# Two changes in a planner's hints: when the first batch's last z tiles are let go, and how soon a block's gate matmuls may run

## The chip, the cores and the metric

The kernel runs on one core of a Trainium2 chip. The metric is the device time of one execution, in microseconds; the median of the runs counts.

## The reference

Attention with a squared-ReLU score is multiplied by `u`, and its rows go through a top-1 mixture of experts with a capacity.

```python
scores = (1 / S) * z @ z.T                # B=8, S=3072, d_qk=64
attn = maximum(scores, 0) ** 2
x = (u * (attn @ v)).reshape(B * S, D)    # D=256
logits = x @ w_gate                       # E=8 experts
expert_idx = argmax(logits, axis=1); gate_w = softmax(logits)[expert_idx]
# each expert takes its first cap = 768 rows, in the order of the tokens
h = maximum(disp @ w1, 0)                 # F=1024
y = h @ w2
out[i] = gate_w[i] * y[expert_idx[i], pos[i]] if kept, else 0
```

## The kernel before

**Work.** Since an expert takes only 768 rows, the kernel computes the attention of the first 14 blocks of 512 rows (`NB0`); blocks 0 to 5 are the first batch, 6 to 11 the second, 12 and half of 13 the third. A flag `more` says whether an expert is still short of rows; only then the second half of block 13, and what follows, is computed. In the runs here that branch isn't taken.

**A block** goes over 12 *pairs* of 128 keys. For each pair six matmuls give the scores (L867, tile `sc`, made for two pairs at a time), ScalarE takes ReLU and square (L884, L889), VectorE splits the result in a high and a low float16 part (L893, L902, tile `hl`), and 24 matmuls sum it with `v` (L993, tile `acc`). The scores are symmetric: what a later block needs again is written to DRAM (`kept`, L914) and loaded transposed (`ld`, L840).

**Key tiles.** The scores read `zz`, which holds z^T as high and low parts. For the first batch, tiles 0 to 11 (three groups of four) are made on TensorE: split by ScalarE and VectorE (L401, L404, L405), turned (L416), copied out (L422). Pairs 4 and 5 of block 0 read group 2. Tiles 12 to 23, read from pair 6 on, go another way: loaded a second time (`zlate`, L440), split six tiles at a time (`z_wide`: L449 on ScalarE, L452 on VectorE), turned by two DMA transposes (L456), and the two halves swapped by two more DMAs (L464).

**A block's route.** When a block's sums are done (L943, `x`), VectorE scales its rows (L651 and what follows), they are split (L663, L666) and turned by DMA (L674, `xt`); 16 gate matmuls (L681, `lg`) give the logits, VectorE takes the argmax (L692 to L697), five small matmuls count (L702 to L708, `cum`), VectorE makes slots, counts and the gate weight (L738 to L748, L721 to L726), and GpSimd scatters the rows to `disp` with four indirect DMAs (L84). For block 13 it is half of all that.

**Experts.** For a slab of rows, `fxt` is loaded transposed from `disp` by SP (L1088), L1132 makes the hidden layer (`hps`), L1117 and L1118 split it, L1154 multiplies by w2 (`yps`), L1160 scales, and GpSimd scatters the rows to `out` (L84). Expert 0 comes in slabs of 512, 128 and 128 rows, the others in one of 768. The first two slabs of expert 0 are loaded while block 12 runs. After the 512 rows, all engines read `more` (L1264) and pass the branch of L1265; behind it GpSimd runs one instruction that replaces the semaphore counts of the scatters that were skipped. The third slab and expert 1's are loaded after that.

**What sets the order.** Each engine works through its instructions in the order written. That order is made at build time: `Chain` holds stages of work for other engines, and between the matmuls of TensorE `weave` emits from each chain what fits. A chain isn't touched before its `gate` is in `done`; `("pair", p)` is set when the sums of pair p begin. A chain of rank -2 may put work on ScalarE and VectorE at any time. One of rank -1 may do so before pair 3 only where the engine's planned backlog is at most 0.2 us. Chains of lower rank come first. A chain's item for TensorE is emitted when the planner's clock has passed `ready + lag`:

```python
            if eng == "PE":
                return self.ready + self.lag <= now
...
                if self.rank < 0:
                    return self.rank < -1 or ("pair", 3) in done or t - now <= 0.2
```

`lag` is `LAG` = 4.5 (us of the planner) for the routes of all blocks but the last ones. The planner's microseconds are not measured times.

Of the kernel before, what the change touches and what calls it, by code (L numbers as in the profile page):

```python
# [26 lines left out]
def attention_moe_kernel(ctx: ExitStack, tc: tile.TileContext, u, v, z, w_gate, w1, w2, out, cap):  # L27
# [6 lines left out]
    JT = S // P  # L34
# [110 lines left out]
    def warm_up(n):  # L145

        t = ps.tile([P, BLK], F32, tag="acc", name="warm", bufs=3)
        for _ in range(n):
            op("PE", 0.2155)
            nc.tensor.matmul(t, lhsT=ones, rhs=ones.unsqueeze(1).to_broadcast([P, BLK // P, P]), start=True, stop=True)  # L150
# [22 lines left out]
    LAG = 4.5  # L173
# [4 lines left out]
    done = {}  # L178
# [10 lines left out]
    def op(eng, cost, dep=0.0):  # L189
        start = max(clk[eng], dep + HOP)  # L190
        if eng in ("SP", "XB"):
            start = max(clk["SP"], dep + HOP)
            clk["SP"] = start + (0.5 if eng == "SP" else max(1.2, 0.3 + cost))
            clk["DMA"] = max(clk["DMA"], start + 1.4) + cost
            return clk["DMA"] + 1.0
        clk[eng] = start + cost
        return clk[eng]
# [118 lines left out]
    def tag():  # L316
        uid[0] += 1
        return uid[0]
# [12 lines left out]
    def prepare(bt, first=False):  # L331
# [102 lines left out]
        ZW = 6  # L434

        NT = 3 * 4 if first else 0
# [5 lines left out]
        def z_wide(t0):  # L442
            st = Bag()
            k = min(ZW, JT - t0)
            src = (lambda: bt.zlate[:, t0 - NT:t0 - NT + k]) if first else (lambda: bt.zraw[:, t0:t0 + k])

            def hi():
                st.zhl = sb.tile([P, ZW, 2, DQ], F16, tag="zhl", name="zhl", bufs=3)
                nc.scalar.activation(st.zhl[:, 0:k, 0, :], src(), AF.Copy, scale=bt.zs)  # L449

            def lo():
                nc.vector.scalar_tensor_tensor(out=st.zhl[:, 0:k, 1, :], in0=src(), scalar=bt.zs,  # L452
                                               in1=st.zhl[:, 0:k, 0, :], op0=ALU.mult, op1=ALU.subtract)

            def tr():
                nc.sync.dma_start_transpose(  # L456
                    out=bt.zz[:, 0, t0 * P:(t0 + k) * P].rearrange("p (t q) -> p t q", q=P),
                    in_=st.zhl[:, 0:k].rearrange("p t h d -> p (t h d)"))

            return [[("ACT", 0.5, hi, None)], [("DVE", 0.48, lo, None)], [("XB", 0.68, tr, None)]]  # L460

        def z_swap(h):
            def f():
                nc.sync.dma_start(out=bt.zz[DQ * (1 - h):DQ * (2 - h), 1, NT * P:],  # L464
                                  in_=bt.zz[DQ * h:DQ * (h + 1), 0, NT * P:])
                if h:
                    for g in range(NT // 4, ZG):
                        done[key("z", g)] = clk["DMA"] + 1.0
            return ("SP", 1.2, f, key("z", NT // 4) if h else None)
# [28 lines left out]
        def v_piece(t0, k):  # L498
            o, i, a = slice(t0, t0 + k), t0 // 4, t0 % 4

            def hi():
                nc.scalar.activation(bt.v2[:, o, 0, :], bt.vraw[i][:, a:a + k], AF.Copy, scale=bt.vs)

            def lo():
                nc.vector.scalar_tensor_tensor(out=bt.v2[:, o, 1, :], in0=bt.vraw[i][:, a:a + k], scalar=bt.vs,
                                               in1=bt.v2[:, o, 0, :], op0=ALU.mult, op1=ALU.subtract)
                for j in range(t0 + 2, t0 + k, 2):
                    done[key("v", j // 2)] = clk["DVE"]

            return [[("ACT", 0.19 + 0.21 * k, hi, None)], [("DVE", 0.06 + 0.285 * k, lo, key("v", t0 // 2) if t0 + k > t0 // 2 * 2 + 1 else None)]]  # L510
# [12 lines left out]
        def pipe(groups):  # L523

            n = max(len(g) + i for i, g in enumerate(groups))
            return [[it for i, g in enumerate(groups) if 0 <= s - i < len(g) for it in g[s - i]] for s in range(n)]

        if first:
# [5 lines left out]
            late = op("SP", 2.0)  # L534
# [23 lines left out]
        def need_max(k, n):  # L558
            return max(done[key(k, i)] for i in range(n))
# [13 lines left out]
        def go(c, n=1):  # L573
            for _ in range(n):
                assert c.item() is not None
                c.emit()
# [16 lines left out]
        def to_sums(follow):  # L593

            G[1] = Chain(z_group(1), -2, done[key("s")])
            go(A[2])
            go(follow[0], 3)
            go(A[3])
            go(follow[0], 2)
            go(G[1])  # L600
            go(A[4])
            go(follow[1], 2)
            go(A[6])
            go(G[1])
            go(A[5])
            warm_up(14)
            go(G[1])
            warm_up(8)
            vr = Chain([[("DVE", 0.2, v_red, None)], [("POOL", 0.4, v_all, None)], [("DVE", 0.6, v_bits, key("vs"))]], -2,
                       need_max("m", NM))  # L610
            go(vr, 2)
            go(G[1], 2)
            go(vr)
            for t, k in ((0, 1), (1, 1), (2, 2)):
                V[t] = Chain(v_piece(t, k), -2, done[key("vs")])
            go(V[0])
            go(V[1])
            go(V[0])
            go(V[1])
            go(follow[1])  # L620
            go(V[2])
            go(follow[1], 2)
            go(V[2])
            Chain(z_group(2), -1, done[key("s")], gate=("pair", 0))
            Chain(pipe([z_wide(t0) for t0 in range(NT, JT, ZW)]) + [[z_swap(0), z_swap(1)]], -1, late, gate=("pair", 1))
            for i in range(2, JT // 2):
                Chain(v_piece(2 * i, 2), -2, done[key("vs")], gate=("pair", i - 2))

# [181 lines left out]
    def attention(blocks, hook):  # L810

        NP = len(blocks) * NPAIR
        prs, acc, xs, ut, sct, sq, corner = {}, {}, {}, {}, {}, {}, {}
# [132 lines left out]
        def start_route(n, rid):  # L946
            bt, _, _, cc = blocks[n]
            keys = [(aid, "x", n, h) for h in range(cc // 2)]
            watchers.append((lambda: all(k in done for k in keys), lambda: route(
                xs.pop(n), bt, max(done[k] for k in keys), LAG if n < len(blocks) - 2 else 0.5, cc, rid)))  # L950

        loads_to(1)
        bt = blocks[0][0]
# [6 lines left out]
        for p in range(NP):  # L960
            n, g = divmod(p, NPAIR)
            bt, ib, c0, cc = blocks[n]
# [8 lines left out]
            for c in range(cc):  # L971
# [7 lines left out]
                if g == 0 and c % 2 == 0:  # L979

                    k = bank[0] - 3
# [17 lines left out]
            if g == NPAIR - 1:  # L999
                need(bt.key("f"), "init")  # L1000
                acc.pop(n)
                ut.pop(n)
                rid = tag()
                last_route[0] = [(rid, "sc", c) for c in range(cc)], (rid, "cnt")
                start_route(n, rid)
# [202 lines left out]
    with tc.manual_schedule():  # L1208
# [4 lines left out]
        for b, bt in bats.items():  # L1213
            n = min(BPB, NB0 - b * BPB)
# [58 lines left out]
        blocks = [(bats[n // BPB], n % BPB, 0, CC if n < NB0 - 1 else CC // 2) for n in range(NB0)]  # L1273
# [59 lines left out]
```

## Time and profile before

| | |
|---|---|
| three runs | 799.09, 800.66, 807.9 us |
| median | 800.66 us |
| profiled execution | 804.33 us |
| its span, first to last instruction | 802.6 us |
| TensorE busy (matmuls) | 778.2 us, 97% of the span |
| VectorE, ScalarE, GpSimd busy | 493.0, 402.9, 115.9 us |

The attention ends at about 538 us of the span, the experts fill the rest. The profiled execution is 1.7 us longer than its span and 3.7 us above the median.

### The profile page before, as it was taken

Reading aid. Unit: us, or ns where it says so; the run is one execution under the profiler, and the core shown is the slowest. Engines: PE = TensorE matmul, PEld = TensorE weight load, DVE = VectorE, ACT = ScalarE, POOL = GpSimd, SP = SyncE. Lnnn points to the kernel's source line nnn. Section 1 sums busy time; section 2 is a strip of 40 time slices with the busy share of each in tenths; the row PEclk is TensorE's granted clock in tenths of the full one; section 3 lists DMA queues with packets and bytes.
Section 4 is the critical chain, followed back from the end, with each engine's and each line's share of the span. In section 5 each row is a group of like instructions: output and inputs, shape, how many; then the busy total and the mean of one; then the engine's idle time right before and its main releaser. Section 6 shows DMA issues by size and latency. Waiting matters only on the chain. (4 is left out here: it accounts for less than half of the span.)

```text
span 802.6 us, 17029 instructions
## 1 busy us (share of the span) xinstructions
PE 778.2 (97%) x6857; PEld 607.8 (76%) x6857; DVE 493.0 (61%) x1080; ACT 402.9 (50%) x692; POOL 115.9 (14%) x122
## 2 busy tenths in 40 slices
PE   8899999999999999999999999998999999999996
PEld 3587878788877777888688877866776877867865
DVE  6877888453526979874525269885674473564540
ACT  6877565322216748452413058553664464564541
POOL 0000010120102010101101010104121312312202
PEclk9999999999999999999999999999999999999998
DMA  7499999999998997889699989861997846845001
GB/s 216 140 221 283 243 210 238 184 246 177 223 192 206 279 232 228 193 195 227 160 223 208 195 203 253 285 182 43 198 329 266 294 131 260 233 153 170 27 15 44
DMA packets 287069, 160.60 MB, mean 200 GB/s; under 512 B 227341, under 2 KB 253274, under 8 KB 286976
## 3 DMA queue, kind: packets, MB, share of 16 engines
q1 hardware_dynamic: 282080, 146.58, 74.1%
q0 software_dynamic: 4896, 12.79, 4.9%
q8 instruction: 57, 0.93, 0.5%
q14 instruction: 36, 0.29, 0.1%
HBM read 36.25 MB, written 71.46 MB: 134 GB/s over the span
## 5 line engine op out<-in xcount | busy, mean ns | idle before, releaser
L993 PE MATMUL acc<-v,hl 128*128 128x256 f16 x2280 | 259.5, 273 | 0.7 <-DVE hl L902 0.4
L993 PEld LDWEIGHTS <-hl 128*128 128x128 f16 x2280 | 219.7, 98 | 34.9 <-issue 4.6
L884 ACT ACTIVATE r<-sc 128x512 f32<-128x512 f32 (+1 forms) x212 | 105.6, 550 | 151.8 <-PE sc L867 150.1
L993 PE MATMUL acc<-v,ld 128*128 128x256 f16 x1464 | 167.9, 274 | 4.1 <-DMA ld<-kept 2.8
L993 PEld LDWEIGHTS <-ld 128*128 128x128 f16 x1464 | 141.9, 98 | 26.8 <-issue 6.3
L1132 PE MATMUL hps<-fxt,wt 128*128 128x384 f16 (+2 forms) x816 | 128.1, 320 | 3.8 <-PEq L1265 2.4
L1154 PE MATMUL yps<-wt,hh 128*128 128x256 f16 x1152 | 128.0, 273 | 0.0
L1118 DVE SCALAR_TENSOR_TENSOR hh<-hps,hh 128x384 f16<-128x384 f32 (+2 forms) x136 | 71.1, 532 | 90.6 <-ACT hh L1117 89.5
L1154 PEld LDWEIGHTS <-hh 128*128 128x128 f16 x1152 | 112.5, 98 | 14.1
L902 DVE TENSOR_TENSOR hl<-a,hl 128x1024 f16<-128x1024 f32 (+1 forms) x106 | 118.2, 1115 | 3.6
L1132 PEld LDWEIGHTS <-wt 128*128 128x128 f16 x816 | 77.2, 99 | 52.6 <-issue 4.4
L84 POOL DMA_INDIRECT disp<-xr,slot x54 | 56.5, 1045 | 336.8 <-ACT r L884 129.3
L889 ACT ACTIVATE a<-r 128x1024 f32<-128x1024 f32 (+1 forms) x106 | 102.6, 968 | 2.5
L893 DVE CAST hl<-a 128x1024 f16<-128x1024 f32 (+1 forms) x106 | 67.6, 638 | 55.3 <-ACT a L889 55.1
L1117 ACT ACTIVATE hh<-hps 128x384 f16<-128x384 f32 (+2 forms) x136 | 63.2, 470 | 51.6 <-PE hps L1132 50.6
L867 PE MATMUL sc<-zz 64*128 64x512 f16 (+1 forms) x636 | 72.0, 356 | 2.6 <-DMA zz<-zz 1.9
L84 POOL DMA_INDIRECT out<-ys,sid x48 | 53.1, 1107 | 128.0 <-ACT ys L1160 85.3
L1160 ACT ACTIVATE ys<-yps,sg 128x256 f32<-128x256 f32 x48 | 22.7, 473 | 76.1 <-PE yps L1154 69.9
L663 ACT ACTIVATE xr<-x,rsr 128x256 f16<-128x256 f32 x54 | 25.2, 502 | 68.9 <-DVE rsr L60 66.2
L867 PEld LDWEIGHTS <-zz 64*128 64x128 f16 x636 | 26.9, 94 | 36.4 <-issue 10.7
L943 DVE TENSOR_TENSOR x<-acc,u 128x512 f32<-128x512 f32 x27 | 18.6, 689 | 46.8 <-PE acc L993 43.2
L1061 DVE SCALAR_TENSOR_TENSOR wt<-wraw,w1r,wt 128x1024 f16<-128x1024 f32 (+1 forms) x18 | 20.4, 1163 | 12.9 <-ACT wt L1057 12.8
(126 smaller groups left out, 420.6 us busy)
## 6 DMA issues: line engine op xcount, KB each, us to landing
kept<-hl SPq DMA_DIRECT2D x62, 512.0 KB
out<-zero SPq DMA_DIRECT2D x48, 512.0 KB
wraw<-in_moe_w SPq DMA_DIRECT2D x32, 512.0 KB
vraw<-in_v SPq DMA_DIRECT2D x18, 512.0 KB
u<-in_u SPq DMA_DIRECT2D x13, 512.0 KB
zraw<-in_z SPq DMA_DIRECT2D x2, 768.0 KB
zz<-zz SPq DMA_DIRECT2D x4, 384.0 KB
ld<-kept SPq DMA_TRANSPOSE x62
```

The costliest lines, as they stand in the source:

```text
L84: r = nc.gpsimd.indirect_dma_start(out=dst, out_offset=bass.IndirectOffsetOnAxis(ap=idx, axis=0), in_=src, in_offset=None, bounds_check=bo ...
L663: return lambda: nc.scalar.activation(st.x16[:, c, 0:D], st.x[:, c, :], AF.Copy, scale=st.rs[:, c:c + 1])
L867: nc.tensor.matmul(s[jj][:, 0:w], lhsT=bt.zz[rows, (kl + jj) % 2, j * P:(j + 1) * P], rhs=bt.zz[rows, (ql + jj) % 2, q0:q0 + w], start=(i ...
L884: nc.scalar.activation(sct[p][:, jj, :], s[jj][:, 0:w], AF.Relu)
L889: nc.scalar.activation(sq[p], sct.pop(p), AF.Square)
L893: nc.vector.tensor_copy(hl[:, :, :, 0, :], sq[p].rearrange("p j (t k) -> p j t k", k=HB))
L902: nc.vector.tensor_sub(hl[:, :, :, 1, :], a.rearrange("p j (t k) -> p j t k", k=HB), hl[:, :, :, 0, :])
L993: nc.tensor.matmul(o, lhsT=a(h, jj, c), rhs=bt.v2[:, j, l], start=(j + h + l + c % 2 == 0), stop=(j == JT - 1 and h == 1), skip_group_chec ...
L1117: Chain([[("ACT", 0.05 + w * 0.00083, lambda: nc.scalar.activation(th, src, AF.Relu), None)], [("DVE", 0.07 + w * 0.00104, lambda: nc.vect ...
L1118: [("DVE", 0.07 + w * 0.00104, lambda: nc.vector.scalar_tensor_tensor(out=tl, in0=src, scalar=0.0, in1=th, op0=ALU.max, op1=ALU.subtract), ...
L1132: nc.tensor.matmul(o, lhsT=wx.w1[:, d, wp, f * P:(f + 1) * P], rhs=sx.xt[:, xp * DC + d, a:a + w], start=(q == 0), stop=(q == len(seq) - 1))
L1154: nc.tensor.matmul(y, lhsT=hid(i, f)[:, sl], rhs=w[:, l], start=(f + i + l == 0), stop=(f == FC - 1 and i == 1))
```

## The change

The chain of the wide z tiles of the first batch gets rank -2 in place of -1 and waits for pair 0 in place of pair 1. The short lag of 0.5 holds for the last block (13, a half block) only; block 12 gets 4.5.

```diff
@@ to_sums @@
-            Chain(pipe([z_wide(t0) for t0 in range(NT, JT, ZW)]) + [[z_swap(0), z_swap(1)]], -1, late, gate=("pair", 1))
+            Chain(pipe([z_wide(t0) for t0 in range(NT, JT, ZW)]) + [[z_swap(0), z_swap(1)]], -2, late, gate=("pair", 0))
@@ start_route @@
-                xs.pop(n), bt, max(done[k] for k in keys), LAG if n < len(blocks) - 2 else 0.5, cc, rid)))
+                xs.pop(n), bt, max(done[k] for k in keys), LAG if n < len(blocks) - 1 else 0.5, cc, rid)))
```

No instruction is added or taken away; the order moves. On ScalarE at the start of block 0, while the sums of pairs 0 and 1 run, this stood before (`v_318` is the split v, `a` the squares, `zhl` the split z; L449 are the two wide splits):

```order
L889 ACTIVATE a<-r 128x1024
L502 ACTIVATE v_318<-vraw,vsr 128x2x256 x2
L401 ACTIVATE zhl<-zraw,zb_205 128x4x64
L884 ACTIVATE r<-sc 128x512 x2
L889 ACTIVATE a<-r 128x1024
L884 ACTIVATE r<-sc 128x512
L502 ACTIVATE v_318<-vraw,vsr 128x2x256
L449 ACTIVATE zhl<-zlate,zb_205 128x6x64
L422 COPY zz<-ztp 128x2x2x128
L884 ACTIVATE r<-sc 128x512
L889 ACTIVATE a<-r 128x1024
```

and this stands there now:

```order
L889 ACTIVATE a<-r 128x1024
L502 ACTIVATE v_318<-vraw,vsr 128x2x256
L449 ACTIVATE zhl<-zlate,zb_205 128x6x64
L502 ACTIVATE v_318<-vraw,vsr 128x2x256
L449 ACTIVATE zhl<-zlate,zb_205 128x6x64
L401 ACTIVATE zhl<-zraw,zb_205 128x4x64
L884 ACTIVATE r<-sc 128x512 x2
L889 ACTIVATE a<-r 128x1024
L502 ACTIVATE v_318<-vraw,vsr 128x2x256
L884 ACTIVATE r<-sc 128x512 x2
L422 COPY zz<-ztp 128x2x2x128
```

Both wide splits now stand ahead of group 2's split (L401) and of the ReLUs of pairs 2 and 3; group 2's copy (L422) has both ahead of it, and one ReLU more. VectorE's wide residues (L452) move the same way, and its first copies of `tri`, `wt8` and the gate weights move behind block 0's pairs.

On SP, the DMA queue, from the loads of block 0 on (`kept_0_1` is what block 0 writes for block 1):

```order
 L440 DMA zlate<-in_z 128x12x64
-L914 DMA kept_0_1_88<-hl 128x2x1024
 L456 DMA_TRANSPOSE zz<-zhl 128x6x128 x2
-L914 DMA kept_0_1_88<-hl 128x2x1024
 L464 DMA zz<-zz 64x1536 x2
+L914 DMA kept_0_1_88<-hl 128x2x1024 x2
 L914 DMA kept_0_2_89<-hl 128x2x1024 x2
-L305 DMA disp<-dinit 6144x1x8
 L914 DMA kept_0_3_91<-hl 128x2x1024 x2
```

The transposes and swaps of the wide tiles pass the first two writes of `kept`. In block 1, three of the second batch's six loads of v (L360) move behind other transfers, and the loads of `ld` for block 2 each stand behind one transpose less of the second batch's z (L456), from the second on.

On GpSimd, from the rows of blocks 11 and 12 to the branch (`disp` are scatters of a block's rows, `out` those of the first slab's results, `wma` a reduction for expert 1's weights):

```order
 L84 DMA disp<-xr,slot 6144x264 x8
-L77 ISA wma<-wm_7882 128x2
+L84 DMA out<-ys,sid 24576x256
+L77 ISA wma<-wm_7949 128x2
 L84 DMA out<-ys,sid 24576x256
 L84 DMA disp<-xr,slot 6144x264 x2
-L84 DMA out<-ys,sid 24576x256 x3
+L84 DMA out<-ys,sid 24576x256 x2
 L1264 TENSOR_LOAD more
 L1265 COMPARE_AND_BRANCH
```

One scatter to `out` passes the reduction, and block 13's two scatters to `disp` fall one place back. On TensorE, block 12's 16 gate matmuls move from before the last 36 sums of block 13 to behind them, directly ahead of expert 0's first product; its five counting matmuls move from among those sums to behind the 30th of the 48 hidden products; block 13's gate matmuls move from behind the third of the first slab's 96 output products to behind the 15th. On VectorE the second part of block 12's route (argmax, slots, counts, gate weight) moves from ahead of block 13's last L943 to behind it, among the splits of the hidden layer.

## Rows read from the trace of the kernel before

**Rows 1.** Timeline of TensorE, block 0: start, length, instruction, [wait before <-releaser].

```profile
28.05 1.47 PE L867 MATMUL sc<-zz 64*128 64x512 f16 x12 [0.51 <-DVE zz L422]
...
32.82 2.58 PE L993 MATMUL acc<-v,hl 128*128 128x256 f16 x22 [0.36 <-DVE hl L902]
35.33 0.39 PE L867 MATMUL sc<-zz 64*128 64x512 f16 x1
37.62 1.78 PE L867 MATMUL sc<-zz 64*128 64x512 f16 x11 [1.91 <-DMA zz<-zz]
```

**Rows 2.** Timeline of SP in block 0: the wide tiles' two transposes.

```profile
30.56 2.66 SPq L456 DMA_TRANSPOSE zz<-zhl  x2
```

**Rows 3.** Timeline of ScalarE in block 0.

```profile
20.89 1.32 ACT L502 ACTIVATE v<-vraw,vsr 128x512 f16<-128x512 f32 x2
...
25.80 0.60 ACT L449 ACTIVATE zhl<-zlate,zb 128x384 f16<-128x384 f32 x1
26.30 0.73 ACT L422 COPY zz<-ztp 128x512 f16<-128x512 f16 x1
```

**Rows 4.** Timeline of VectorE in block 0.

```profile
27.26 0.73 DVE L422 COPY zz<-ztp 128x512 f16<-128x512 f16 x1
...
31.02 0.61 DVE L452 SCALAR_TENSOR_TENSOR zhl<-zlate,zb,zhl 128x384 f16<-128x384 f32 x1
```

**Rows 5.** Stretches: busy times of the engines, granted clock, DMA share, GB/s.

```profile
17.00:18.00 1.00, 0.69 (x10) 0.60 (x11) 0.89 (x4) 0.71 (x4) 0.00 (x0) 1.00 0.00 0
...
386.00:388.00 2.00, 2.00 (x12) 1.39 (x10) 1.83 (x7) 0.93 (x1) 0.00 (x0) 0.50 0.64 85
```

**Rows 6.** Timeline of TensorE: end of the attention, and the first three experts' slabs.

```profile
533.82 0.26 PE L681 MATMUL lg<-wg,xt 128*128 128x16 f16 x4 [1.21 <-DMA xt<-xr]
...
537.98 10.53 PE L1132 MATMUL hps<-fxt,wt 128*128 128x512 f16 x48
...
561.64 4.21 PE L1132 MATMUL hps<-fxt,wt 128*128 128x128 f16 x48 [2.35 <-PEq L1265]
...
575.64 6.66 PE L1132 MATMUL hps<-fxt,wt 128*128 128x384 f16 x40 [0.58 <-DMA fxt<-disp]
```

**Rows 7.** Timeline of SP behind the branch: third slab, then expert 1's.

```profile
563.34 1.22 SPq L1088 DMA_TRANSPOSE fxt<-disp  x1
...
566.58 6.69 SPq L1088 DMA_TRANSPOSE fxt<-disp  x1
```

**Rows 8.** Line L1265 on GpSimd's sequencer: count, shortest/median/longest ns, start.

```profile
L1265 POOLq INC_SWDGE_SEM  x1: 1351/1351/1351, 561.8 to 561.8; - x1
```

**Rows 9.** Timeline of GpSimd at the first slab.

```profile
539.41 0.97 POOL L84 DMA_INDIRECT disp<-xr,slot  x1 [20.29 <-DVE x L943]
540.69 0.97 POOL L84 DMA_INDIRECT disp<-xr,slot  x1 [0.30 <-issue]
...
547.76 0.37 POOL L77 PARTITION_ALL_REDUCE wma<-wm  x1 [3.54 <-DVE wm L1036]
...
560.93 0.97 POOL L84 DMA_INDIRECT out<-ys,sid  x1 [1.30 <-ACT ys L1160]
```

**Rows 10.** Timeline of VectorE: second part of block 12's route, then the first slab.

```profile
534.11 0.23 DVE L692 TENSOR_REDUCE lgs<-lg 128x32 f32<-128x64 f32 x1 [0.89 <-PE lg L681]
...
536.53 0.19 DVE L738 TENSOR_TENSOR pq<-oh,cum 128x32 f32<-128x32 f16 x1 [0.97 <-PE cum L708]
...
538.55 0.69 DVE L943 TENSOR_TENSOR x<-acc,u 128x512 f32<-128x512 f32 x1
...
545.79 1.21 DVE L73 TENSOR_REDUCE wm<-wraw 128x1 f32<-128x1024 f32 x1
546.92 0.68 DVE L1118 SCALAR_TENSOR_TENSOR hh<-hps,hh 128x512 f16<-128x512 f32 x1
```

**Rows 11.** Timeline of TensorE in block 2, and in the second batch.

```profile
110.67 2.79 PE L993 MATMUL acc<-v,ld 128*128 128x256 f16 x24 [1.30 <-DMA ld<-kept]
...
385.32 0.28 PE L681 MATMUL lg<-wg,xt 128*128 128x16 f16 x4 [1.83 <-DMA xt<-xr]
385.45 4.38 PE L993 MATMUL acc<-v,ld 128*128 128x256 f16 x24
```

## The prediction

> **What bounds the kernel now.** I read the table of engines first: TensorE is busy for 778.2 of 802.6 us, so only its gaps can be won, and of those only the ones whose end isn't set by something else. Then I listed its waits in order of time, and for each looked up on the releasing engine's timeline what stood ahead of the releaser. The two edits touch two stretches.
>
> At the start, the scores of pairs 6 and 7 begin at 35.33, stop after one matmul, and wait 1.91 us for the swaps of the wide key tiles [rows 1]. With the wait they take until 37.62 + 1.78 = 39.40, so 4.07 us from 35.33 on, where the twelve of pairs 4 and 5 take 1.47 [rows 1]: the late tiles cost 2.6 us. The chain behind it is short: VectorE's second residue starts at 31.02 and ends at 31.63 [rows 4], SP turns [rows 2], swaps, and TensorE goes on at 37.62, 6.0 us after that residue. Two smaller waits come just before: 0.51 us for the copy of group 2, and 0.36 us for the split of pair 3 [rows 1].
>
> At the end of the attention, block 12's gate matmuls hold TensorE up for 1.21 us, as the transposed rows aren't there; then come the last sums, the first slab from 537.98, the branch (2.35 us), and at 575.64 expert 1, which waits only 0.58 us for its slab [rows 6]. That last wait is the one to look at. Expert 1's load is issued at 566.58, after the third slab's at 563.34 [rows 7], and the third slab's waited for GpSimd: its instruction behind the branch ends at 561.8 + 1.35 = 563.15 [rows 8], and that one comes after the last scatter of the first slab, which starts at 560.93 [rows 9]. So for the time from 561 to 576 GpSimd and SP set the end, and TensorE's slack against them is 0.58 us.
>
> **The first edit.** ScalarE meets the first wide split behind one piece of v, at about 20.89 + 1.32/2 = 21.5 [rows 3]. Its data are there: no DMA moves anything from 17 to 18 us [rows 5], so the second load of z has landed. Both splits then precede VectorE's residues. ScalarE paces an instruction of this kind by 0.50 us (25.80 to 26.30) [rows 3], so the second split ends at about 21.5 + 0.5 + 0.6 + 0.6 = 23.2, with a piece of v between. VectorE has its share of that piece, a residue of 0.61 [rows 4] and the end of pair 1's split to do before the second residue; I take 2.1 us after ScalarE, 25.3 (an estimate; the cover below is twice that). By the 6.0 us from above the tiles are ready at 31.3. The scores that need them come at 35.3 or later, so there are 4 us of cover, and the 2.6 us go. That the transposes now pass two writes of `kept` only helps.
>
> What is late next is group 2, the key tiles of pairs 4 and 5. Ahead of ScalarE's copy (26.30) [rows 3] there is now one wide split more, 0.50 us, and one ReLU more, half a microsecond: 27.3. On VectorE the copy began at 27.26 [rows 4]; ahead of it come two residues of 0.61 [rows 4], while one result of pair 2 and one of v stand in another order: about 28.25. Both copies are then done 1.0 us later, and pairs 4 and 5 start at 29.05 in place of 28.05. I can't see whether ScalarE's order costs pair 2's split more than that; the bounds are 0.5 (the split alone) and 1.7 us (both splits and the residues' 1.2 in a row, partly hidden). TensorE being a microsecond later, the 0.36 us for pair 3 are covered. From pair 4 on, ScalarE and VectorE need less time per pair than TensorE and catch up.
>
> Sum at the start: -2.6 + 1.0 - 0.4 = **-2.0 us**, between -1.0 and -2.6.
>
> **Between the two places** the order of SP's queue is moved in block 1: three loads of v come later, nearer to the loads for block 2, and the third of these, for which TensorE waits 1.30 us at 110.67 [rows 11], stands behind one transpose less. If all that feeds this load moves 2 us earlier along with TensorE, the wait stays as it is. Nothing in the trace shows it in the new order, so I bound it: the wait vanishes (-1.3), or the load lands when it did and the wait takes all of TensorE's lead (+2.0). I take 0, since those transfers are issued behind the pairs' own results. From block 3 on SP's order is the same as before.
>
> **The second edit.** Block 12's gate matmuls leave their place, and the wait of 1.21 us goes: when they come again, ahead of 537.98, their data have been there for 3 us. The matmuls themselves only change places. So the first slab starts 1.2 to 1.3 us earlier. Within the slab VectorE has block 12's second part on top: from 534.11 to 538.55, less a wait of 0.97, 3.5 us [rows 10]. It holds up the hidden layer's splits, and TensorE may lose between nothing and 1 us there, in waiting for the last split or for block 13's counts.
>
> GpSimd decides, not that. Block 12's rows can be scattered only when their gate weight is written. VectorE starts block 13's L943 at about 536.6 (in the old clock, without the gain of the start). Up to the gate weight it has what stood from 538.55 to 545.79, 7.24 us, two more splits of some 0.6 us, and the 3.5 us: 12 us, so 548.6. Before, the scatter followed the end of that work by 0.86 us (538.55 to 539.41) [rows 9, 10]: now 549.4 in place of 539.41. From there GpSimd has no gap: nine scatters and the reduction stand ahead of the slab's last scatter. From start to start a scatter takes 1.28 us (539.41 to 540.69) [rows 9], nine 11.5, the reduction 0.37 [rows 9] and a gap of 0.3: 549.4 + 12.2 = 561.6, where it started at 560.93. Third slab and expert 1's load follow at fixed distances, 0.6 us later, and expert 1's products begin at 576.2. TensorE arrives earlier and waits longer: the 1.2 us are spent there. Nothing after that moves.
>
> Here a rule of the Trainium skill decides how to count. The row gives 0.97 us for a scatter and 1.28 from start to start [rows 9]. The Trainium skill, Perfetto Trace Analysis, section "GPSIMD Engine Instruction", says that a GpSimd instruction's span in a profile is unreliable and that one should go by the spacing of starts. Counted by spans the nine would take 8.7 us and the last scatter would be ready at 558.8, so that it would again wait for its data and the sum at the end would be -1.2; counted by the page's rule it is the 561.6 above.
>
> Sum at the end: **+0.6 us**, between -1.2 (GpSimd keeps up) and +2.0 (VectorE's list takes a microsecond and a half more).
>
> **Sum.** -2.0 + 0 + 0.6 = -1.4. Against the profiled execution's own 804.33 that is 802.9; carried over to the median of 800.66, 3.7 us below it, **799.3 us**. The difference, 0.17%, is within 1%, about what a measurement of this kernel can tell from no change.
>
> **The rivals.**
>
> *The end keeps its gain.* If block 12's rows come to GpSimd two microseconds sooner than I count, or the scatters run at their spans' pace, the last scatter waits for its data as before, everything up to expert 1 moves 1.2 us ahead, and the time is 800.66 - 2.0 - 1.2 = 797.5. For it: the list on VectorE holds work for which I have only pieces of rows. Against it: the four scatters in a row at 1.28.
>
> *The load for block 2 takes the lead back, and the clock with it* (slower than before). Three loads of v now fall nearer to the loads for block 2. If the third of these lands no earlier than it did, TensorE's 2.0 us become a wait of 3.3 in place of 1.30 at that point. In this trace a wait of 1.83 us at 385.32 [rows 11] was followed by a granted clock of 0.50 (1.2 GHz) from 386 to 388 [rows 5], and the next 24 sums took 4.38 us [rows 11] in place of 2.79 [rows 11], 1.6 us more. With that: 800.66 - 2.0 + 2.0 + 1.6 + 0.6 = 802.9. It decides from the point at which the load comes later than 110.67 less the lead. Against it: the loads are queued behind the pairs' results, which do come earlier.
>
> *The change doesn't do what it says*: ScalarE, now stopping for the second load of z at 21.5, stands still and holds pair 2 up. The empty DMA engines at 17 us speak against it; with it the start would gain nothing, 801.3.
>
> **How the numbers follow.** Forecast 0.55, the end's gain kept 0.2, the slower rival 0.2, the third 0.05. The forecast's own bounds are 800.66 - 2.6 + 0.6 = 798.7 to 800.66 - 1.0 + 2.0 = 801.7; the first rival at its best (-2.6 - 1.2) gives 796.9, the second 802.9. Range with half a microsecond at either end for the median of three runs: 796.4 to 803.4. No case comes near 1%: faster by more 0.03, within 0.94, slower 0.03.
>
> **What would show it.** In the changed trace: the wait for `zz<-zz` of the wide tiles gone and the one for L422 about 1.5 us; the sums of pair 4 starting at about 37.3 in place of 39.4; no wait for `xt` at the end of the attention; GpSimd without gaps from the first of block 12's scatters to the slab's last; the wait for expert 1's slab about 2 us in place of 0.58. I am wrong if group 2's wait swallows the start's gain, if the wait in block 2 grows, or if GpSimd has gaps.

## The result, and the profile after

The changed kernel takes 806.08 us (median of 20 runs, 802.59 to 812.17), the kernel before 800.5 in the same rounds: a ratio of 1.0065, 95% interval 1.0046 to 1.0083, so by the ratio 5.2 us slower. That is within 1%, but it lies 2.7 us above the range. The profiled execution of after took 805.91 us (span 804.1), near its median. That of before took 804.33, 3.8 above its own, so the two executions differ by 1.6 us only. A second profiled execution of before, at 800.63 us, is used below where the first was unlucky.

**The start is as predicted.** Timeline of TensorE in block 0, after:

```profile
29.09 1.47 PE L867 MATMUL sc<-zz 64*128 64x512 f16 x12 [1.36 <-DVE zz L422]
...
35.84 1.47 PE L867 MATMUL sc<-zz 64*128 64x512 f16 x12
37.24 2.79 PE L993 MATMUL acc<-v,hl 128*128 128x256 f16 x24
```

The wait for the wide tiles [rows 1] is gone, the one for group 2 has grown to 1.36 us, and the sums of pair 4 start at 37.24.

**Block 2 takes it back.** Timeline of TensorE, after: the gate matmuls of blocks 0, 1, 2 and 11, and the longest wait between them.

```profile
84.29 0.55 PE L681 MATMUL lg<-wg,xt 128*128 128x16 f16 x16
...
107.19 2.72 PE L993 MATMUL acc<-v,ld 128*128 128x256 f16 x12 [5.32 <-DVE x L943]
...
128.63 0.55 PE L681 MATMUL lg<-wg,xt 128*128 128x16 f16 x16
160.85 0.46 PE L681 MATMUL lg<-wg,xt 128*128 128x16 f16 x12
...
499.82 0.55 PE L681 MATMUL lg<-wg,xt 128*128 128x16 f16 x16
```

At 107.19 block 2's sums wait 5.32 us for VectorE's L943, which empties the banks of block 1. The twelve sums behind the wait take 2.72 us in place of 1.47, and the granted clock of the stretch 108 to 112 us is 0.70. The third load for block 2, for which before waited 1.30 us [rows 11], is no longer waited for. What holds L943 up is read on ScalarE and on VectorE. Timeline of ScalarE, after:

```profile
105.27 0.61 ACT L449 ACTIVATE zhl<-zraw,zb 128x384 f16<-128x384 f32 x1 [10.83 <-DMA zz<-zhl]
```

Timeline of VectorE, after:

```profile
105.92 0.62 DVE L452 SCALAR_TENSOR_TENSOR zhl<-zraw,zb,zhl 128x384 f16<-128x384 f32 x1 [7.51 <-ACT zhl L449]
106.46 1.28 DVE L943 TENSOR_TENSOR x<-acc,u 128x512 f32<-128x512 f32 x2
```

ScalarE's fourth wide split of the second batch needs one of three `zhl` buffers, and the first comes free when the first wide transpose has landed. VectorE waits 7.51 us for that split, and L943 stands behind. That transpose is late on SP. Timeline of SP, before (second profile), then after:

```profile
42.27 0.64 SPq L305 DMA_DIRECT2D disp<-dinit  x1
...
62.78 0.46 SPq L354 DMA_DIRECT2D zraw<-in_z  x1
63.30 4.13 SPq L360 DMA_DIRECT2D vraw<-in_v  x2
68.97 2.50 SPq L908 DMA_TRANSPOSE corner<-hl  x2
```

```profile
57.66 0.65 SPq L305 DMA_DIRECT2D disp<-dinit  x1
58.40 4.26 SPq L354 DMA_DIRECT2D zraw<-in_z  x1
63.88 4.80 SPq L908 DMA_TRANSPOSE corner<-hl  x2
68.72 1.68 SPq L360 DMA_DIRECT2D vraw<-in_v  x3
...
81.35 1.89 SPq L360 DMA_DIRECT2D vraw<-in_v  x2
...
99.86 1.57 SPq L456 DMA_TRANSPOSE zz<-zhl  x1
```

The zero rows of `disp` (L305), which the diff of SP's order shows leaving their place in block 0, come back here, right ahead of the second batch's z; two loads of v that stood ahead of block 1's corner transposes now stand behind them.

**At the end** block 12's wait is gone, and others come. Timeline of TensorE, after (`fps` is the sum of the counts from which `more` is made, L1265 the branch):

```profile
536.42 6.63 PE L1132 MATMUL hps<-fxt,wt 128*128 128x512 f16 x30
...
555.55 0.18 PE L778 MATMUL fps<-cnt,ones 128*128 128x8 f16 x1 [1.77 <-DVE s L741]
...
563.30 4.31 PE L1132 MATMUL hps<-fxt,wt 128*128 128x128 f16 x48 [3.30 <-ACTq L1265]
...
578.14 15.76 PE L1132 MATMUL hps<-fxt,wt 128*128 128x384 f16 x96 [1.42 <-DMA fxt<-disp]
```

The first slab starts 1.56 us earlier than before and expert 1 2.50 us later [rows 6]. Two of the waits weren't there, or were shorter, before: 1.77 us ahead of `fps` and 3.30 in place of 2.35 at the branch. For the first, VectorE's timeline, after:

```profile
551.49 0.16 DVE L713 TENSOR_TENSOR ex<-d,rfg 128x16 f32<-128x16 f32 x1
554.37 0.17 DVE L738 TENSOR_TENSOR pq<-oh,cum 128x16 f32<-128x16 f16 x1 [2.72 <-PE yps L1154]
```

TensorE's last counting matmul, which L738 reads, starts at 551.62 and takes 0.17. VectorE stands idle for 2.6 us more, with nothing queued ahead of L738. GpSimd's timeline, after, shows what else runs then:

```profile
548.62 0.97 POOL L84 DMA_INDIRECT disp<-xr,slot  x1 [28.80 <-DVE sg L58]
549.90 0.98 POOL L84 DMA_INDIRECT disp<-xr,slot  x1 [0.30 <-issue]
...
553.74 0.98 POOL L84 DMA_INDIRECT out<-ys,sid  x1 [0.30 <-issue]
554.75 0.36 POOL L77 PARTITION_ALL_REDUCE wma<-wm  x1
556.62 1.03 POOL L84 DMA_INDIRECT out<-ys,sid  x1 [1.51 <-ACT ys L1160]
```

The scatters of block 12 begin at 548.62 and follow each other by 1.28 us; before they lay at 539 to 544, ahead of all this [rows 9]. And GpSimd has gaps of 1.5 us, so it isn't the length of its list that decides.

**A ledger.** TensorE's timeline gives four lengths that can be compared between kernels: from the turning of key group 1 (the eight L416 at 17.42 in after, at 16.9 to 18.1 in the others) to block 0's gate matmuls (start), from there to block 2's, from there to block 11's, and from there to expert 1's first product (end). All in us, from one profiled execution each; the time of that execution, then the median of the runs.

```
kernel                         start  blk 1-2  blk 3-11   end   profiled  median
before                         69.07   71.81    341.20   76.25   804.33   800.5
before, second profile         71.44   69.63    337.26   75.92   800.63
after                          66.87   76.56    338.97   78.32   805.91   806.08
e1  first edit alone           66.87   77.02    339.22   76.33   805.23   805.23
e2  second edit alone          70.75   69.57    337.59   78.08   801.59   803.16
e3  after, fourth buffer       66.85   75.15    339.26   79.71   806.97   805.8
e4  late constants, no edit    70.73   78.74    341.03   75.92   813.32   810.85
e5  first edit, early consts   66.86   69.74    337.38   76.20   795.20   796.45
e6  e5 and a lag of 1.6        67.02   69.57    337.21   75.02   795.18   795.92
e7  e2, scatters held          70.09   69.74    336.36   80.60   803.81
e8  both edits, early consts   67.02   69.57    339.79   80.12   802.67   800.31
e9  e1, zero rows not booked   66.86   70.40    338.81   76.19   796.63   801.61
e11 e9, second profile         66.86   72.97    339.03   76.14   799.83
e10 early constants alone      70.05   69.58    336.19   77.33   799.08   800.82
```

### The profile page after: what moved, and what is told of

The parts are those of the page before. It is cut to its first block, busy times and chain, and to the rows that moved or that the text cites. A ratio compares the mean times of both kernels' runs of the same rounds, so it can differ in the third digit from the quotient of the medians.

```text
span 804.1 us, 17023 instructions
## 1 busy us (share of the span) xinstructions
PE 776.0 (97%) x6857; PEld 607.6 (76%) x6857; DVE 492.8 (61%) x1080; ACT 403.9 (50%) x692; POOL 116.0 (14%) x122
## 5 line engine op out<-in xcount | busy, mean ns | idle before, releaser
L943 DVE TENSOR_TENSOR x<-acc,u 128x512 f32<-128x512 f32 x27 | 18.4, 688 | 44.6 <-PE acc L993 44.6
```

## The experiments

**Each edit alone, and before once more.** The three kernels are before as it is, before with the first hunk of the diff, and before with the second.

> The kernel before once more, for a second profiled execution: the first one took 804.33 us, 3.8 above the median. If that one lost its time by chance in single waits (block 2's third load, the wait of 1.83 us at 385.32 with the clock of 0.50 behind it), this one ends near 800.5 with those waits smaller and no other work moved. If the profiler itself costs the 3.8 us, it is near 804 again.

> The first edit alone (the wide tiles' chain with rank -2 from pair 0; block 12's lag as before). Theory A, the middle: the start gains 2 us as predicted, then TensorE waits 5.3 us at block 2 for VectorE's product L943, which stands behind the second batch's fourth wide residue, which waits for ScalarE's fourth wide split, which waits for a buffer that the first wide transpose on SP frees; so 802 to 805 us (+1.5 to +4 against before), with that wait in the trace. Theory B, the second edit carries the loss: 797 to 800.

> The second edit alone (block 12's gate matmuls with the long lag). Theory A: the wait of 1.21 us goes, but block 13's counts come late on VectorE, TensorE waits before its counting matmul and in the branch, and expert 1 starts later: 801.5 to 803.5 (+1 to +3). Theory B, the second edit carries the whole loss: 804.5 to 806.5. By the prediction (+0.6 at the end): 801.

Before, again: 800.63 us, with no wait in block 2 nor at 385 us, so the 1.30 and 1.83 us of [rows 11] were chance. But its start took 2.4 us longer than in the first profile. Timeline of TensorE, before, second profile:

```profile
39.29 2.63 PE L867 MATMUL sc<-zz 64*128 64x512 f16 x11 [1.95 <-DMA zz<-zz]
```

The wait for the wide tiles is the same 1.9 us as in [rows 1], but the eleven scores behind it take 2.63 us in place of 1.78. The granted clock of 40 to 44 us is 0.64 here, 0.67 and 0.78 in two other kernels without the first edit (e2, e4), and 1.00 in the other three; with the first edit it is 1.00 each time. So in three of six executions the wait is followed by a fall of TensorE's clock.

That is not all of the 2.4 us. The clock also fell earlier. Stretch of before, second profile:

```profile
20.00:22.00 2.00, 2.00 (x8) 0.99 (x7) 1.25 (x3) 2.00 (x4) 0.00 (x0) 0.50 0.00 0
```

Here, in e7 and in e10 TensorE had waited 2.28 to 2.44 us for key group 1, and the granted clock of 20 to 22 us is 0.50 to 0.59; in before, e2 and e4, which waited 1.08 to 1.43, it is 1.00. The scores of pairs 4 and 5 then start 11.7 us after that turning in place of 10.7. In e6 and e8, which have the first edit, the clock falls there as well (0.50 and 0.55), but TensorE then waits 0.61 us for group 2 in place of 1.36, and their start of 67.02 is within 0.2 us of the others with that edit.

The first edit alone takes 805.23 us (ratio 1.0059, interval 1.0033 to 1.0085), with a wait of 5.66 us for L943 in block 2: theory A's loss, most of the whole. Timeline of TensorE, e1:

```profile
108.10 2.72 PE L993 MATMUL acc<-v,ld 128*128 128x256 f16 x12 [5.66 <-DVE x L943]
```

The second edit alone takes 803.16 (1.0025, 0.9996 to 1.0054). By the median that is 2.2 us, what theory A expects, though the interval reaches down to no change; in its trace TensorE waits 3.27 us before `fps`.

**A buffer more.** After, with the fourth wide tile of a later batch in another buffer:

```diff
-                st.zhl = sb.tile([P, ZW, 2, DQ], F16, tag="zhl", name="zhl", bufs=3)
+                st.zhl = (sb.tile([P, ZW, 2, DQ], F16, tag="fxt", name="zhl") if t0 == 3 * ZW else
+                          sb.tile([P, ZW, 2, DQ], F16, tag="zhl", name="zhl", bufs=3))
```

> The changed kernel, with the fourth wide tile of a later batch in another buffer (one that is free in the attention), so that its split needs no transpose to have landed first; nothing else changes. Theory A: block 2's wait of 5.3 us for L943 goes or shrinks below 1.5 us, and the time falls by 2.5 to 4.5 us against the changed kernel, to 801.5 to 803.5. Rival (the loads for block 2 are late anyhow and take the wait's place, or the clock is the cause): the wait turns into one for a load of about the same length, 805 to 806.5.

805.8 us, the time of after (1.0054, 1.0028 to 1.008). The wait for L943 is gone, as theory A said, and others stand in its place. Timeline of TensorE, blocks 1 and 2:

```profile
109.83 2.79 PE L994 MATMUL acc<-v,ld 128*128 128x256 f16 x24 [2.49 <-DMA ld<-kept]
...
125.92 0.26 PE L682 MATMUL lg<-wg,xt 128*128 128x16 f16 x4 [0.51 <-DMA xt<-xr]
126.53 0.26 PE L682 MATMUL lg<-wg,xt 128*128 128x16 f16 x4 [0.35 <-DMA xt<-xr]
127.84 0.26 PE L682 MATMUL lg<-wg,xt 128*128 128x16 f16 x4 [1.05 <-DMA xt<-xr]
```

So the buffer was only the place where the delay showed. All that SP's queue brings to block 2 is late, and theory A's middle falls; its rival, the late loads, is right in this. The next question is why they are late. Stretches of before's second profile, then of after (busy us of TensorE, its weight loads, VectorE, ScalarE, GpSimd; granted clock, DMA share, GB/s):

```profile
44.00:48.00 4.00, 4.00 (x38) 2.65 (x36) 3.10 (x4) 3.69 (x6) 0.00 (x0) 1.00 0.89 75
...
60.00:64.00 4.00, 4.00 (x38) 3.33 (x37) 0.41 (x1) 0.00 (x0) 0.00 (x0) 1.00 1.20 341
64.00:68.00 4.00, 4.00 (x41) 3.21 (x38) 1.57 (x3) 3.20 (x6) 0.00 (x0) 1.00 1.18 253
68.00:72.00 4.00, 4.00 (x37) 2.65 (x36) 3.90 (x6) 1.10 (x3) 0.00 (x0) 1.00 1.16 310
```

```profile
60.00:64.00 4.00, 4.00 (x39) 3.58 (x37) 2.67 (x4) 3.04 (x6) 0.00 (x0) 1.00 0.76 63
64.00:68.00 4.00, 4.00 (x37) 2.65 (x36) 3.47 (x9) 1.93 (x3) 0.00 (x0) 1.00 1.17 214
68.00:72.00 4.00, 4.00 (x39) 3.40 (x38) 2.79 (x5) 3.73 (x8) 0.00 (x0) 1.00 0.62 141
```

In before's second profile the DMA engines are full from 56 us until 112, at shares from 0.96 to 1.37 but for one stretch (0.56 at 84 to 88). In after this time has two holes: from 60 to 64, behind the zero rows, and from 68 to 72, behind SP's wait for the corners. In these eight us 0.82 MB are moved ((63 + 141) x 4), where before moved 2.6. (Before is some 4 us behind after there; e5 below, whose start is that of after, moves 1.85 MB.) The first hole exists in before too, at 44 to 48, where the share is below one anyway.

**SP's order, with the edits taken apart.** SP's order follows the planner's chain of constants (`tri`, `wt8`, the zero rows), which the first edit pushes back on VectorE. e4 pushes it back without the edits; e5 makes the first edit and pulls it forward; e6 adds a lag of 1.6 for block 12; e9 makes the first edit and lets the planner book no DMA time for the zero rows, so that they stay late but the loads of v go ahead of the corners again (with them other loads of v, a transpose of z and VectorE's work on v move some places); e10 pulls the chain forward without the edits.

```diff
@@ e4
-        Chain([[("DVE", 1.2, more_consts, "consts")], [("DVE", 0.8, prep_gate, "gate")]], 4, 40.0)
+        Chain([[("DVE", 1.2, more_consts, "consts")], [("DVE", 0.8, prep_gate, "gate")]], 4, 44.0)
@@ e5, e6, e8, e10
-        Chain([[("DVE", 1.2, more_consts, "consts")], [("DVE", 0.8, prep_gate, "gate")]], 4, 40.0)
+        Chain([[("DVE", 1.2, more_consts, "consts")], [("DVE", 0.8, prep_gate, "gate")]], -2, 38.0)
-              4, clk["PE"] + 1.0, gate="consts")
+              -2, clk["PE"] + 1.0, gate="consts")
@@ e6
-                xs.pop(n), bt, max(done[k] for k in keys), LAG if n < len(blocks) - 2 else 0.5, cc, rid)))
+                xs.pop(n), bt, max(done[k] for k in keys), LAG if n < len(blocks) - 2 else 1.6 if n < len(blocks) - 1 else 0.5, cc, rid)))
@@ e9
-        Chain([[("DVE", 0.3, fill, None)], [("DVE", 0.3, mark, None)], [("SP", 4.0, put, "init")]],
+        Chain([[("DVE", 0.3, fill, None)], [("DVE", 0.3, mark, None)], [("SP", 0.0, put, "init")]],
```

> The kernel before with neither edit; only the planner's chain of constants (tri, wt8, the zero rows of disp) is due at 44 in place of 40, with which SP's queue comes out as in the changed kernel from the second key pairs on: the zero rows stand right ahead of the second batch's z, and the first two loads of v behind block 1's corner transposes. Theory C, SP's order in block 1: the DMA engines stand half idle from 60 to 72 us while SP waits for the corners, what they didn't move is missing in a stretch in which they are full until 112 us, and block 2 pays: 803 to 806 us with no edit made. Rival (the early wide tiles themselves, or the wide split's buffer, cost it): 800 to 801.5.

> The first edit alone, with the chain of constants at rank -2 from 38 and the zero rows at rank -2, so that SP's queue is that of the kernel before from the zero rows on, and only the wide tiles' transposes stand earlier. Theory C: the loss of the first edit goes and its gain at the start remains, 798 to 800, no wait above 1.5 us in block 2, and DMA at 250 GB/s or more from 60 to 72 us. Rival (the early wide tiles themselves): 803 to 806 as with the first edit alone.

> The same with a lag of 1.6 for block 12 (before 0.5, the changed kernel 4.5): its gate matmuls come twelve sums later than before, its counting matmuls still ahead of the first slab. If the wait of 1.07 to 1.8 us for the transposed rows is all that is to be won at the end, and the lag's loss comes from block 12's second part lying in the slab, this is 0.8 to 1.2 us faster than the kernel sent beside it: 797 to 799. Rival (time won ahead of the slab is spent in the wait for expert 1's slab): no difference.

> The first edit alone; the zero rows of disp stay where the change put them, right ahead of the second batch's z, but the planner books no DMA time for them (0 in place of 4.0), and with that the two loads of v stand ahead of block 1's corners again, as before. If it is the loads of v behind the corners (the DMA engines idle while SP waits): 796 to 799, no long wait in block 2. If it is the zero rows' own 6144 small pieces at that place: 803 to 806, as the first edit alone.

> The control: the kernel before with neither edit, and only the chain of constants early (rank -2 from 38, zero rows rank -2). If the gain of the kernel with the first edit and early constants is the first edit's, this takes what before takes, 800 to 802, with the wait of 1.9 us for the wide tiles still there. If it is the constants' place: 796 to 798.

e4, with neither edit, takes 810.85 us (1.0104, 1.0063 to 1.0144), more than after itself. TensorE waits at the same place:

```profile
111.83 2.72 PE L993 MATMUL acc<-v,ld 128*128 128x256 f16 x12 [6.64 <-DVE x L943]
```

It has the loss of SP's order and not the gain of the start: behind block 0's first writes of `kept`, SP's order is after's, transfer for transfer. e5 is the reverse, with before's order there: 796.45 us (0.9938, 0.9917 to 0.9959), 4.5 us faster than before and 8.8 faster than the same edit in e1, with no wait in block 2. Stretches of e5:

```profile
60.00:64.00 4.00, 4.00 (x39) 3.58 (x38) 2.48 (x4) 3.23 (x6) 0.00 (x0) 1.00 1.16 253
64.00:68.00 4.00, 4.00 (x37) 2.66 (x36) 3.65 (x10) 1.75 (x3) 0.00 (x0) 1.00 1.15 306
68.00:72.00 4.00, 4.00 (x38) 3.44 (x36) 2.60 (x5) 3.73 (x8) 0.00 (x0) 1.00 1.38 209
```

e10, the control, takes 800.82 us (1.0011, 0.9992 to 1.003): the constants' place alone is worth nothing that shows, the gain is the first edit's. e9 takes 801.61 (1.0004, 0.9981 to 1.0028), between e1 and e5: with the loads of v back in place 3.6 us come back, and 5.2 stay lost. Its profiled execution was its shortest, with 0.52 us of waiting in block 2, so it was profiled again.

> The kernel with the first edit and no DMA time booked for the zero rows once more, for a second profile: its first profiled execution took 796.63 us, the shortest of its twelve times, while most lie from 800 to 804. If the zero rows' place costs the difference, an execution near 802 shows TensorE's wait in block 2 grown from 0.52 to 2 us and more, with the clock's fall behind it; if the loss lies elsewhere, block 2 is as before and the time is lost later.

That execution took 799.83 us. Timeline of TensorE, block 2, and a stretch:

```profile
102.87 1.47 PE L993 MATMUL acc<-v,ld 128*128 128x256 f16 x12 [1.03 <-DVE vm L73]
...
109.98 2.79 PE L993 MATMUL acc<-v,ld 128*128 128x256 f16 x24 [1.84 <-DMA ld<-kept]
```

```profile
60.00:64.00 4.00, 4.00 (x39) 3.60 (x37) 2.70 (x4) 3.00 (x6) 0.00 (x0) 1.00 0.78 83
```

It lost 2.6 us more between blocks 0 and 2 than the first one, in these waits, of which the second is for the load. The clock didn't fall, against the expectation. The hole behind the zero rows is there (83 GB/s), and that behind the corners is filled (272 GB/s from 68 to 72). So the order behind the corners makes up part of the loss; that the rest of it is the zero rows' alone isn't shown, since the constants on VectorE are late there as well.

e6 takes 795.92 us (0.9933, 0.991 to 0.9955), faster than both kernels of this study. Against e5 its end is 1.2 us shorter in the ledger, as expected, of which 0.5 us shows in the medians, less than their intervals.

**The second edit on a sound middle, and GpSimd's part.** e8 is both edits with the early constants. e7 is the second edit alone with block 12's scatters held on GpSimd until block 13 has been counted; the order of the other engines is that of e2, instruction for instruction:

```diff
-            [("POOL", 1.04, r_sc(c), (rid, "sc", c)) for c in range(cc)],
+            [("POOL", 1.04, r_sc(c), (rid, "sc", c)) + hold for c in range(cc)],
...
+            done["counted", len(counted)] = clk["DVE"]
+            counted.append(1)
...
+                xs.pop(n), bt, max(done[k] for k in keys), LAG if n < len(blocks) - 1 else 0.5, cc, rid, (("counted", NB0 - 1),) if n == NB0 - 2 else ())))
```

> Both edits of the change, with the chain of constants early as in the kernel with the first edit and early constants, so that SP's queue is that of before from the zero rows on. If the change's loss is the first edit's SP order plus some 2 us of the second edit, this is 2 us slower than that kernel (796.45): 797.5 to 799.5, faster than before though it holds the change whole, and with VectorE's pause before L738 and a wait at fps in its trace. If the second edit costs nothing once the middle is right: 796 to 797.

> The second edit alone, with block 12's four scatters held on GpSimd until block 13's counts are done; the other engines' order is the same. In the kernels with the second edit VectorE's L738 starts 2.5 to 4 us after the counting matmuls that it reads, and ScalarE's ys as late. Theory D (GpSimd's scatters run just then and hold the two engines or their signals up): L738 starts within 1.0 us of the counting matmuls, TensorE's wait before fps goes, and the slab's end pays instead for the later scatters. Rival (it lies in TensorE's order, not in GpSimd): the pause stays at 2.5 to 4 us.

e8 takes 800.31 us (0.9999, 0.998 to 1.0017), 3.9 more than e5: the second edit costs about that where the middle is sound, twice what I expected. The ledger agrees: the end takes 78.1 to 80.6 us in all kernels with the second edit and 75.9 to 77.3 in those with the lag of before.

e7: VectorE's timeline of e2, then of e7.

```profile
551.43 0.17 DVE L738 TENSOR_TENSOR pq<-oh,cum 128x16 f32<-128x16 f16 x1 [4.22 <-remote]
```

```profile
546.73 0.17 DVE L739 TENSOR_TENSOR pq<-oh,cum 128x16 f32<-128x16 f16 x1 [0.17 <-PE cum L709]
```

With the scatters out of the way the pause of 4.22 us is 0.17, and `fps` starts 2.05 us after the first counting matmul (546.46 to 548.51) in place of 5.49 (547.12 to 552.61), without a wait. In the other kernels with the second edit VectorE's pause is 2.72 (after), 3.87 (e3) and 4.20 us (e8). So the pause comes with GpSimd's scatters, as far as one execution of each shows it; how they bring it about isn't shown. It isn't won, though: they now run later, from 547.45 to 557.4 in one row, and hit ScalarE. Timeline of ScalarE, e7, the last scaling of the slab, and of TensorE at the branch:

```profile
559.04 0.47 ACT L1163 ACTIVATE ys<-yps,sg 128x256 f32<-128x256 f32 x1 [6.05 <-remote]
```

```profile
560.09 4.86 PE L1135 MATMUL hps<-fxt,wt 128*128 128x128 f16 x48 [7.13 <-ACTq L1268]
```

TensorE's products of that slab end at 552.96, so this scaling is 6 us late; ScalarE comes to the branch after it, and TensorE waits 7.13 us for ScalarE there.

## Why the prediction was wrong

**The first edit's start** was right in mechanism: ScalarE found its data, the wide tiles came in time, group 2's copy was a microsecond later, pair 3's wait was covered, and the start got 2.2 us shorter than in the trace that I had (69.07 to 66.87), against -2.0. (The bounds written for it, -1.0 and -2.6, don't follow from the 0.5 and 1.7 above them, which give -2.5 and -1.3; nothing hangs on that.) The term was still mis-sized for the kernel as it usually runs. The six profiles without the edit average 70.4 in the ledger, so the gain is 3.5. The one that I worked from had the full clock all through. In the others a lower clock at 20 us (e7 and e10, 70.1), behind the wait for the wide tiles (e2 and e4, 70.7), or at both places (the second profile, 71.4) costs 1.0 to 2.4 us, and with the first edit neither shows in the start.

**"I take 0" between the two places is the step that failed.** The bounds were -1.3 and +2.0; the ledger gives +4.8 against the first profile of before, and +6.5 against the mean of the five profiles with before's order on SP and without the first edit (70.1). Three things went wrong. I looked for a wait at the one load that waited before, which was chance. I bounded a loss by TensorE's lead, as if all that feeds block 2 could at worst come when it did; but it came later than before, since SP's new order left the DMA engines underused for eight microseconds of a stretch in which they are full. And I didn't price a row that I showed: the zero rows' departure from block 0 on SP. They had to stand somewhere else, and the planner, which books 4 us of DMA for them, then held two loads of v back behind the corners. e4 and e5 show that this order, not the early wide tiles, makes the loss; e9 shows that the loads of v are part of it.

The rival that the load for block 2 takes the lead back, and the clock with it, was nearest. Its outcome was right and its price too small for the same reason: 5.32 us of waiting, not 3.3.

**The end** was forecast at +0.6 between -1.2 and +2.0, and measures +2.1 (78.32 against 76.25), +1.8 in e2 (78.08) and +3.9 in e8 (against e5). The 1.2 us of block 12's wait went as said, and were lost again as said. "GpSimd decides, not that" fails as put: it has gaps of 1.5 us, and the wait for expert 1's slab is 1.42 us and not 2. The first scatter came at 548.62, where 549.4 was counted (without the gain of the start), and the pace was the 1.28 us from start to start that I chose. The Trainium skill, Perfetto Trace Analysis, section "GPSIMD Engine Instruction", has one go by the spacing of starts, and the trace agrees on that: 548.62 to 549.90 in after. What I didn't see is that the scatters now run while VectorE and ScalarE wait for TensorE's results, and that both pause there. The loss reaches TensorE through `fps` and the branch, not through the slab's last scatter.

Together: -3.5 at the start, +6.5 in the middle and +2.1 at the end make +5.1, where 5.2 were measured. Reckoned in the same way, e2 comes to +1.3 (middle -0.5, end +1.8; 2.2 measured) and e5 to -3.8 (start -3.5, middle -0.3; -4.5 measured). That 5.1 lies so near to 5.2 is luck: the sum leaves out blocks 3 to 11, where after has 338.97 and the same five profiles between 336.19 and 341.20, 337.7 on average, so another +1.2 that nothing here explains.

## What to carry to other kernels

When an edit lets work go earlier, follow in the order what it pushes back, down to transfers that nobody waits for: a small DMA of many pieces in a full stretch of the queue, or a load behind a transpose that must wait, delays everything that the queue brings later, and the wait shows far from its cause. Removing the buffer at which such a delay shows can move the wait and not end it, as in e3. And profile the starting point twice before a wait is priced, since its price can include a fall of the clock that one execution has and the next has not.

## What the runs showed of the hardware

- The zero rows are 6144 pieces of 32 bytes, 0.2 MB. In the four us behind their issue the DMA engines moved 63 to 83 GB/s at shares of 0.76 to 0.89 in before's second profile, after and e11, and in e5, where SP issued nothing else until 42.5 us, 39 GB/s at 0.52 (40 to 44 us). In after the load of z issued behind them held SP for 4.26 us, where it took 0.46 in before's second profile. The Trainium skill, DMA: Bandwidth & Descriptors, section "Why small descriptors are slow (HBM only)", says that each packet and each descriptor has a fixed cost whatever its size; the trace agrees in kind (a busy share of 0.76 for 63 GB/s); no run here measures the cost of one piece.
- While GpSimd issued indirect scatters one behind the other, some of VectorE's and ScalarE's reads of TensorE's results began 2.6 to 6 us after the matmuls had ended, in e2, e3, e7, e8 and after. Others did not: in e7 VectorE read `fps` at 548.75, within 0.1 us of the matmul's end, in the same row of scatters, and in before four scatters in a row ran from 539 to 544 us without such a pause. So it takes more than a row of scatters; what, stays open. Some of these waits end with `<-remote`, a signal at whose time no recorded matmul ends, so it is also open whether the engines answer late or TensorE's signal comes late.
- TensorE's own branch instruction took 3.35 to 4.08 us, against 0.05 to 0.07 us on ScalarE, VectorE and GpSimd (sequencer rows of L1265, all runs). In e6 that instruction ends TensorE's wait at the branch, in after and e7 it is ScalarE's late arrival.
